# Moving two kinds of copies between ScalarE and VectorE, and replacing zero matmuls by wider ones, in an attention-then-MLP kernel

## The chip, the cores and the metric

The kernel runs on one core of one Trainium2 chip. The metric is device time in microseconds for one execution of the whole program; the time of a kernel is the median of several executions. Lower is better.

## The reference, cut to what matters

Eight batches, eight heads of 64, 512 tokens and 32 state rows. Two attentions without projections are computed for each head, one with the tokens as queries (`xread`) and one with the state rows as queries (`sread`), and all resulting rows go through one two-layer MLP with a SiLU.

```python
scores = scale * (x @ state.T)              # 512 x 32 for each batch and head
a = softmax(scores); xread = a @ state
a2 = softmax(scale * (state @ x.T)); sread = a2 @ x
rows = concat([xread, sread], axis=2) -> [4352, 512]
out = silu(rows @ w_in) @ w_out             # w_in 512x2048, w_out 2048x512
```

## The kernel before, in words

**The algebra.** Since `xread = a @ state`, the first MLP layer of a batch is `a @ (state @ w_in)`. So for each batch the kernel makes `W1 = state @ w_in` (`w1_m`, matmuls in line 282, copied out of PSUM by `w1_e`), the transposed softmax `aT`, then `g = silu(W1.T @ aT)` in 16 feature blocks (`g1`: matmuls in line 329, SiLU on ScalarE in line 338), and `out = g.T @ w_out` (`g2`, line 354; `G2` is one feature block for all four token tiles). The state reads of all batches are put through the MLP as a ninth batch (lines 341, 349).

**The softmax of a batch.** The tokens are cast to bf16 (`cast_x`), transposed on TensorE (`x_T`, line 144) and copied out (`x_Te`); `sc` (line 176) makes the scores, `ex` (line 187) the exponentials `en` on ScalarE, a VectorE reduction and a reciprocal give `rs`, and `norm_m`/`norm_g` (lines 202, 214) write the normalised `an`, part on VectorE and part on GpSimd (POOL). `a_T` (line 230) transposes `an` on TensorE into PSUM and copies it to `aT`. `sread_m` (line 246) makes the state reads.

**Order.** The whole schedule is written out by hand: each engine runs its instructions in the order of the Python calls, and a wait holds up all that stands behind it on that engine. `cp(eng, ...)` is the helper that puts a copy on VectorE (line 84), GpSimd (line 86) or ScalarE (line 88), so copies of many kinds share a line number. The eight PSUM banks have names (o0, o1, w0, w1, h0, h1, a0, a1), and a matmul into a bank waits for the copy that last reads it.

**The head (lines 386 to 506).** While the first tokens arrive by DMA, TensorE runs matmuls on a tile of zeros whose result nobody reads: `warm(n, bank, w)` issues n of them, each with its own weight load, w columns wide (128 if nothing is said).

```python
def warm(n, bk, w=128):
    for i in range(n):
        nc.tensor.matmul(bank[bk][:, 0:w], zeros[:, 0:128], zeros[:, 0:w], ...)
```

Then come batch 0's steps: `x_T(0, 0)` on the first two heads, `st_T` (line 124, the state's transpose, copied twice by VectorE into `sbd`), `st_f32` (an f32 copy `sbd_f`, one half on ScalarE), the other three `x_T`, `sc`, `ex`, and the reductions, with three more small `warm` calls between them. The first 512 columns of W1 are made in f32 straight from the loaded weights (`w1f_m`, line 295), in two halves around `a_T(0, ...)`.

**Batch 0 with batch 1 (lines 504 to 595).** `g1` and `G2` of batch 0 are interleaved with W1 pieces of both batches and with the softmax of batch 1. `load_wi(j)` and `load_wo(j)` bring 512-column pieces of the weights by DMAs that GpSimd issues. Near the end of this part ScalarE loads the table for the exponential, runs `ex(1, ...)` twice, loads the SiLU table back, and copies the last W1 piece of batch 0 (`w1_e(0, 3, HB, ...)`, from banks h0 and h1). `g1(0, 12)`, the next user of that piece, writes into bank h1. `a_T(1, ...)` stands behind it on TensorE.

**The rest (from line 598)** is a steady stream: batch k's `g2` matmuls with the next batch's work filled in between at fixed steps.

Of the kernel before, what the change touches and what calls it, by code (L numbers as in the profile page):

```python
# [19 lines left out]
def kernel(  # L20
# [58 lines left out]
    def bf(name):  # L79
        return bank[name][:].bitcast(BF16)  # L80

    def cp(eng, dst, src):
        if eng == "dve":
            nc.vector.tensor_copy(dst, src)  # L84
        elif eng == "pool":
            nc.gpsimd.tensor_copy(dst, src)  # L86
        else:
            nc.scalar.activation(dst, src, func=COPY, bias=0.0)  # L88
# [43 lines left out]
    def st_f32(bk, e0, e1):  # L132
        v = bf(bk)[:, 0:128]
        for half, e in ((0, e0), (1, e1)):
            cp(
                e,
                sbd_f[ds(64 * half, 64)],
                v[ds(64 * half, 64)].rearrange("p (ns kt) -> p kt ns", kt=KT),
            )

    def x_T(b, kt, bk):
        v = bf(bk).rearrange("p (k c t) -> p k c t", k=2, c=4)
        for c in range(4):
            nc.tensor.transpose(
                v[:, kt % 2, c, :], x_n[b % 2][:, kt, c, ds(2, 128)], ident[:]
            )
# [26 lines left out]
    def sc(b, kt, bk):  # L173
        v = bank[bk][:].rearrange("p (k h c s) -> p k h c s", k=2, h=2, c=4)
        for c in range(4):
            nc.tensor.matmul(  # L176
                v[:, kt % 2, :, c, :],
                xT[b % 2][:, kt, c, :],
                sbd[:, b, kt, :, :],
                start=True,  # L180
                stop=True,
                skip_group_check=True,
            )

    def ex(b, kt, n, bk):
        v = bank[bk][:].rearrange("p (k q s) -> p k q s", k=2, q=8)
        nc.scalar.activation(  # L187
            en[b % 2][:, :, :, ds(kt, n), :].rearrange("p h c k s -> p k (h c) s"),
            v[:, ds(kt % 2, n)],
            func=EXP,  # L190
            bias=0.0,
            scale=SCALE,
        )
# [6 lines left out]
    def norm_m(b, eng, kt=0, n=4, h0=0, hn=2):  # L200
        e = nc.vector if eng == "dve" else nc.gpsimd
        e.tensor_tensor(  # L202
            an[b % 2][:, ds(h0, hn), :, ds(kt, n), :].rearrange("p h c k s -> p (h c) k s"),
            en[b % 2][:, ds(h0, hn), :, ds(kt, n), :].rearrange("p h c k s -> p (h c) k s"),
            rs[b % 2][:, ds(h0, hn), :, ds(kt, n)]
            .rearrange("p h c k -> p (h c) k")
            .unsqueeze(3)
            .to_broadcast([128, 4 * hn, n, NS]),
            op=MULT,
        )  # L210

    def norm_g(b, eng, kt, n, q0, qn):
        e = nc.vector if eng == "dve" else nc.gpsimd
        e.tensor_tensor(
            an[b % 2][:].rearrange("p h c k s -> p (h c) k s")[:, ds(q0, qn), ds(kt, n), :],
            en[b % 2][:].rearrange("p h c k s -> p (h c) k s")[:, ds(q0, qn), ds(kt, n), :],
            rs[b % 2][:]
            .rearrange("p h c k -> p (h c) k")[:, ds(q0, qn), ds(kt, n)]
            .unsqueeze(3)
            .to_broadcast([128, qn, n, NS]),  # L220
            op=MULT,
        )

    def a_T(b, bks):
        n = 2 // len(bks)
        for i, (bk, e) in enumerate(bks):
            v = bf(bk).rearrange("p (h c t) -> p h c t", h=2, c=4)
            for half in range(n):
                for c in range(4):
                    nc.tensor.transpose(  # L230
                        v[:, half, c, :], an[b % 2][:, i * n + half, c, :, :], ident[:]
                    )
            cp(e, aT[b % 2][:, ds(i * n, n)], v[:, ds(0, n)])
# [22 lines left out]
    def sread_c(b, bk, o=0, eng="act"):  # L256
        cp(eng, s_f[b % 2][:], bank[bk][:, ds(o, 2 * D + 2)])
# [21 lines left out]
    def w1_m(b, j, bks, kts=range(KT)):  # L279
        for kt in kts:  # L280
            for half in range(2):
                nc.tensor.matmul(  # L282
                    bank[bks[half]][ds(32 * kt, 32), :],
                    sbd[ds(64 * half, 64), b, kt, half, :],
                    w_in_sb[ds(64 * half, 64), kt, ds(512 * j, 512)],
                    start=True,
                    stop=True,
                    skip_group_check=True,
                    tile_position=(64 * half, 32 * kt),
                )  # L290
# [14 lines left out]
    def w1_e(b, j, bks, engs, c0=0, n=512):  # L305
        for half in range(2):
            dst = W1[b % 2][:, half, ds(512 * j + c0, n)]
            src = bank[bks[half]][:, ds(c0, n)]
            if j > 0:
                dst = dst.rearrange("p (c q) -> p c q", c=4)  # L310
                src = src.rearrange("p (q c) -> p c q", c=4)
            cp(engs[half], dst, src)
# [38 lines left out]
    def g2(b, tt, ft, bk, cols=(0, 512)):  # L351
        src = g[b % 2] if b < B else g_s
        c0, c1 = cols
        nc.tensor.matmul(  # L354
            bank[bk][:, c0:c1],
            src[:, ft, ds(128 * tt, 128)],
            w_out_sb[:, ft, c0:c1],
            start=(ft == 0),
            stop=(ft == 15),
            skip_group_check=True,  # L360
        )
# [15 lines left out]
    def warm(n, bk, w=128):  # L377
        for i in range(n):
            nc.tensor.matmul(  # L379
                bank[bk][:, 0:w], zeros[:, 0:128], zeros[:, 0:w], start=True, stop=True,  # L380
                skip_group_check=True,
            )

    with tc.manual_schedule():
# [10 lines left out]
        for i in range(2):  # L395
            nc.vector.memset(x_n[i][:, :, :, 1:131:129], 1.0)
        nc.scalar.preload_act_table(EXP)
        warm(30, "o0")

        XB = ("o0", "o1", "o0", "w1")  # L400
        SB = ("h0", "h1", "a0", "a1")
# [1 line left out]
        HB = ("h0", "h1")  # L403
        OB = ("w0", "w1", "o0", "o1")
        DA = ("dve", "act")
        DD = ("dve", "dve")

        def G2(b, ft):
            for tt in range(4):
                g2(b, tt, ft, OB[tt])  # L410
# [37 lines left out]
        st_T(0, "w0", "dve", "dve")  # L448
        cast2(0, 2)
        st_f32("w0", "act", "dve")  # L450
        warm(3, "w1")
        x_T(0, 1, XB[1])
        x_Te(0, 1, 1, XB[1], "act")
        cast2(0, 3)
# [2 lines left out]
        load_wi(1)  # L457
        sc(0, 0, SB[0])
        ex(0, 0, 1, SB[0])
        warm(4, "w1")  # L460
        sc(0, 1, SB[1])
        ex(0, 1, 1, SB[1])
        x_T(0, 2, XB[2])
# [4 lines left out]
        x_Te(0, 3, 1, XB[3], "dve")  # L468
        rec(0)
        norm_m(0, "pool", 0, 2)  # L470
        warm(2, "o1")
        for kt in (2, 3):
            sc(0, kt, SB[kt])
            ex(0, kt, 1, SB[kt])
# [14 lines left out]
        warm(2, "o1", 512)  # L489
        nc.scalar.preload_act_table(SILU)  # L490
        w1_e(0, 0, ("w0", "w1"), ("act", "dve"), 0, 256)
        a_T(0, (("a0", "dve"), ("a1", "act")))
        sread_c(0, "o0", 0, "dve")
        cp("act", st_nat[:, 1, :], st_f[1][:])
        load_x(1, nc.gpsimd, 2, 2)
# [53 lines left out]
        norm_s(1, 0, 2)  # L549
        norm_m(1, "pool", 0, 2)  # L550
        nc.vector.tensor_reduce(rs[1][:, :, :, 2:4], en[1][:, :, :, 2:4, :], axis=AX, op=ADD)
        nc.vector.reciprocal(rs[1][:, :, :, 2:4], rs[1][:, :, :, 2:4])
        norm_g(1, "dve", 2, 2, 0, 5)
        norm_g(1, "pool", 2, 2, 5, 3)
        G2(0, 9)
        G2(0, 10)
        w1_m(0, 3, HB)
        w1_e(0, 3, HB, ("act", "act"))
        G2(0, 11)
        sread_m(1, "a0")  # L560
        g1(0, 12)
# [164 lines left out]
```

The softmax here doesn't subtract the row's maximum and nothing guards it: scores larger than these inputs give would overflow.

## Time and profile before

| | us |
|---|---|
| median of 5 executions | 215.96 (215.64 to 216.15) |
| the profiled execution | 215.37 |
| span in its trace | 213.6 |
| TensorE matmuls busy | 208.0 (97% of the span) |
| ScalarE busy | 135.6 (63%) |
| VectorE busy | 85.8 (40%) |
| GpSimd busy | 44.6 (21%) |

The span is the part of the profiled execution that the trace covers; 1.8 us lie around it. PE is TensorE's matmuls, PEld its weight loads, DVE is VectorE, ACT is ScalarE, POOL is GpSimd, SP issues most DMAs. In a timeline, each line gives the start and the duration in us, the engine, the source line, the operation, its output and input tiles, and how often it occurs; in brackets stands how long the engine had been idle and what released it. Matmuls overlap: the next one starts before the one before it has ended. In the chain of waits, the work that ended last is followed back from the end, each piece with its start and length. The granted TensorE clock is shown as full (9 in tenths) through the whole span.

### The profile page before, as it was taken

To read this page: it belongs to the slowest core of one execution; us is meant where nothing else is said; L and a number is where in the kernel's file an instruction comes from. 1 tells how busy PE (TensorE), PEld (TensorE's weight loads), DVE (VectorE), ACT (ScalarE), POOL (GpSimd) and SP (SyncE) were. 2 spreads that over 40 slices of the span, in tenths; PEclk is the share of its full clock that TensorE was granted. 3 is DMA by queue.
4 is the path that set the end of the run, shared out by engine and by line. 5 is a ranking of instruction groups with operands and counts; after the bars stand their busy time and mean duration, and the time that the engine had idled before them with its cause. 6 is when DMAs were issued, how large, how long until landed. Compare 5 with 4: busy or idle time off the path is not lost.

```text
span 213.6 us, 4128 instructions
## 1 busy us (share of the span) xinstructions
PE 208.0 (97%) x1666; PEld 104.6 (49%) x1666; DVE 85.8 (40%) x183; ACT 135.6 (63%) x227; POOL 44.6 (21%) x86
## 2 busy tenths in 40 slices
PE   7899999999999999999999999999999999999993
PEld 7544544444454454444444544444444444666553
DVE  4983758706801664076016741382027601111110
ACT  3856686789587668883886477846885476233211
POOL 3686249003400430052005200160001000000000
PEclk9999999999999999999999999999999999999999
DMA  6999997791780197119910891165014101111112
GB/s 200 324 253 271 235 287 76 183 292 68 166 275 9 45 197 248 49 49 155 290 49 0 205 248 48 49 166 129 3 49 112 55 34 49 52 49 49 49 52 98
DMA packets 36803, 27.86 MB, mean 130 GB/s; under 512 B 22064, under 2 KB 31152, under 8 KB 36784
## 3 DMA queue, kind: packets, MB, share of 16 engines
q1 hardware_dynamic: 31872, 21.63, 36.0%
q0 software_dynamic: 4208, 5.44, 12.2%
q10 hardware_dynamic: 704, 0.52, 0.7%
q8 instruction: 13, 0.21, 0.4%
q14 instruction: 6, 0.05, 0.1%
HBM read 17.30 MB, written 8.91 MB: 123 GB/s over the span
## 4 chain that ended last, share of the span: by engine, by line
PE 93%; ACT 3%; DVE 1%; issue 1%; ACTq 0%
PE ps_o L354 28%; PE ps_w L354 26%; PE ps_h L329 26%; PE ps_h L341 3%; PE ps_o L379 2%; PE ps_a L176 1%; ACT en L187 1%; PE ps_h L282 1%; PE ps_o L282 1%; PE ps_o L246 1%; ACT W L88 1%; PE ps_a L282 1%; PE ps_a L329 1%; ACT L548 1%; PE ps_w L282 1%
## 5 line engine op out<-in xcount | busy, mean ns | idle before, releaser
L338 ACT ACTIVATE g<-ps_h 128x512 bf16<-128x512 f32 x125 | 74.1, 597 | 32.5 <-PE ps_h L329 27.9
L354 PEld LDWEIGHTS <-g 128*128 128x128 bf16 x512 | 49.0, 98 | 55.3 <-issue 2.8
L329 PE MATMUL ps_h<-aT,W 128*128 128x512 bf16 x250 | 73.5, 379 | 0.3 <-ACT W L88 0.2
L354 PE MATMUL ps_w<-w_out_sb,g 128*128 128x512 bf16 x256 | 73.0, 379 | 0.1
L354 PE MATMUL ps_o<-w_out_sb,g 128*128 128x512 bf16 x256 | 66.7, 379 | 0.1
L329 PEld LDWEIGHTS <-W 128*128 128x128 bf16 x256 | 24.3, 98 | 27.6 <-issue 1.7
L202 POOL TENSOR_TENSOR an<-en,rs 128x512 bf16<-128x512 bf16 x8 | 8.4, 1053 | 107.9 <-ACT en L187 71.3
L84 DVE COPY o_sb<-ps_w 128x512 f32<-128x512 f32 (+1 forms) x13 | 8.5, 662 | 51.4 <-PE ps_w L354 51.4
L84 DVE COPY o_sb<-ps_o 128x512 f32<-128x512 f32 x14 | 9.5, 687 | 28.6 <-PE ps_o L354 28.5
L86 POOL CAST x_u<-x_f 128x256 bf16<-128x256 f32 x44 | 17.9, 451 | 0.0
L349 ACT ACTIVATE g_s<-ps_h 128x256 bf16<-128x256 f32 x16 | 6.1, 383 | 14.0 <-PE ps_h L341 14.0
L197 DVE TENSOR_REDUCE rs<-en 128x16 f32<-128x512 bf16 x13 | 8.6, 659 | 16.0 <-ACT en L187 15.9
L341 PE MATMUL ps_h<-xsT,w_in_sb 128*128 128x256 bf16 x64 | 9.6, 273 | 0.0
L88 ACT ACTIVATE W<-ps_h 128x512 bf16<-128x512 f32 x11 | 6.5, 598 | 3.7 <-PE ps_h L282 3.7
L341 PEld LDWEIGHTS <-w_in_sb 128*128 128x128 bf16 x64 | 6.9, 110 | 3.7
L88 ACT ACTIVATE o_sb<-ps_o 128x512 f32<-128x512 f32 (+1 forms) x4 | 2.2, 544 | 10.3 <-PE ps_o L354 7.9
L187 ACT ACTIVATE en<-ps_a 128x512 bf16<-128x512 f32 (+1 forms) x16 | 8.4, 568 | 0.5 <-PE ps_a L176 0.4
L176 PEld LDWEIGHTS <-xT 128*128 128x128 bf16 x128 | 5.9, 98 | 4.3 <-ACT xT L88 0.8
L640 ACT ACT_TABLE_LOAD x6 | 7.7, 1283 | 0.1
L187 ACT ACT_TABLE_LOAD x6 | 7.7, 1283 | 0.1
L84 DVE CAST W<-ps_h 128x512 bf16<-128x512 f32 x9 | 6.2, 683 | 4.0 <-PE ps_h L282 4.0
L88 ACT ACTIVATE o_sb<-ps_w 128x512 f32<-128x512 f32 (+1 forms) x5 | 2.7, 533 | 7.8 <-issue 6.2
(90 smaller groups left out, 173.8 us busy)
## 6 DMA issues: line engine op xcount, KB each, us to landing
out_dram<-o_sb SPq DMA_DIRECT2D x32, 256.0 KB, 2.6
x_f<-in_x_dram SPq DMA_DIRECT2D x8, 512.0 KB, 4.9
x_f<-in_x_dram SPq DMA_DIRECT2D x8, 256.0 KB, 4.5
w_in_sb<-in_moe_w_in_dram POOLq DMA_DIRECT2D x3, 512.0 KB, 9.4
w_out_sb<-in_moe_w_out_dram POOLq DMA_DIRECT2D x3, 512.0 KB, 9.5
w_f<-in_moe_w_in_dram SPq DMA_DIRECT2D x2, 512.0 KB, 5.8
wo_f<-in_moe_w_out_dram SPq DMA_DIRECT2D x4, 256.0 KB, 7.2
x_f<-in_x_dram POOLq DMA_DIRECT2D x2, 512.0 KB, 7.7
```

The lines of the kernel that those rows point to most:

```text
L84: nc.vector.tensor_copy(dst, src)
L86: nc.gpsimd.tensor_copy(dst, src)
L88: nc.scalar.activation(dst, src, func=COPY, bias=0.0)
L176: nc.tensor.matmul(v[:, kt % 2, :, c, :], xT[b % 2][:, kt, c, :], sbd[:, b, kt, :, :], start=True, stop=True, skip_group_check=True,)
L187: nc.scalar.activation(en[b % 2][:, :, :, ds(kt, n), :].rearrange("p h c k s -> p k (h c) s"), v[:, ds(kt % 2, n)], func=EXP, bias=0.0, sc ...
L197: nc.vector.tensor_reduce(v, en[b % 2][:, :, :, ds(kt, n), :], axis=AX, op=ADD)
L202: e.tensor_tensor(an[b % 2][:, ds(h0, hn), :, ds(kt, n), :].rearrange("p h c k s -> p (h c) k s"), en[b % 2][:, ds(h0, hn), :, ds(kt, n), ...
L282: nc.tensor.matmul(bank[bks[half]][ds(32 * kt, 32), :], sbd[ds(64 * half, 64), b, kt, half, :], w_in_sb[ds(64 * half, 64), kt, ds(512 * j, ...
L329: nc.tensor.matmul(bks[i][:], W1[b % 2][:, half, ds(128 * (f0 + i), 128)], aT[b % 2][:, half, :, :], start=(half == 0), stop=(half == 1), ...
L338: nc.scalar.activation(g[b % 2][:, f0 + i, :], bks[i][:], func=SILU, bias=0.0)
L341: nc.tensor.matmul(bk[:, 0:256], wi_cols(kt, ft), xsT[:, kt, :, :, :], start=(kt == 0), stop=(kt == KT - 1), skip_group_check=True,)
L354: nc.tensor.matmul(bank[bk][:, c0:c1], src[:, ft, ds(128 * tt, 128)], w_out_sb[:, ft, c0:c1], start=(ft == 0), stop=(ft == 15), skip_group ...
```

## The change

Three edits.

1. The zero matmuls: 30 of 128 columns become 8 of 512; 3 of 128 become 1 of 256; 4 of 128 become 1 of 512; 2 of 128 become 1 of 256. They are 39 before and 11 after, and their columns go from 4992 to 5120. The four other wide ones in the head are untouched.
2. In `a_T(0, ...)` the first half of the transposed softmax (bank a0) is copied by ScalarE and the second (bank a1) by VectorE; it was the other way round.
3. The last W1 piece of batch 0 is copied by VectorE (h0) and ScalarE (h1); both were on ScalarE. To do so the three lines that end batch 1's normalisation (one reciprocal on VectorE, `norm_g` on VectorE, `norm_g` on GpSimd) move behind the calls of `G2(0, 9)`, `G2(0, 10)`, `w1_m` and `w1_e`. On TensorE the order of instructions stays as it was but for the zero matmuls; on GpSimd and SP nothing changes place. On VectorE one copy of 128x512 is put in ahead of the reciprocal.

```diff
-        warm(30, "o0")
+        warm(8, "o0", 512)
...
-        warm(3, "w1")
+        warm(1, "w1", 256)
...
-        warm(4, "w1")
+        warm(1, "w1", 512)
...
-        warm(2, "o1")
+        warm(1, "o1", 256)
...
-        a_T(0, (("a0", "dve"), ("a1", "act")))
+        a_T(0, (("a0", "act"), ("a1", "dve")))
...
         nc.vector.tensor_reduce(rs[1][:, :, :, 2:4], en[1][:, :, :, 2:4, :], axis=AX, op=ADD)
+        G2(0, 9)
+        G2(0, 10)
+        w1_m(0, 3, HB)
+        w1_e(0, 3, HB, DA)
         nc.vector.reciprocal(rs[1][:, :, :, 2:4], rs[1][:, :, :, 2:4])
         norm_g(1, "dve", 2, 2, 0, 5)
         norm_g(1, "pool", 2, 2, 5, 3)
-        G2(0, 9)
-        G2(0, 10)
-        w1_m(0, 3, HB)
-        w1_e(0, 3, HB, ("act", "act"))
         G2(0, 11)
         sread_m(1, "a0")
         g1(0, 12)
         a_T(1, (("a1", "dve"),))
```

`DA` is ("dve", "act").

## The prediction

> **What bounds the kernel now.** I read the page's chain by engine first, then the chain in order of time for the first 32 us, then the timelines of the two places that the change touches, then the waits of TensorE.
>
> ```profile
> PE 93%; ACT 3%; DVE 1%; issue 1%; ACTq 0%
> ```
>
> TensorE carries nearly the whole span. After 12 us it hardly waits: in the stretch 36 to 100 us it is busy 63.81 of 64.00. So a delay or a gain that reaches TensorE at 12 us or at 31 us is carried to the end one for one, unless a wait in between takes it up. The head, in the chain of waits:
>
> ```profile
> 1.19 3.38 PE ps_o L379 x30
> 4.57 0.43 PE ps_o L144 x4
> 5.00 0.12 PE ps_w L124
> 5.12 0.02 issue
> 5.14 0.28 DVE sbd L84
> ```
>
> The 30 zero matmuls are themselves the first link. The first transpose starts at 4.36, right behind them, though its last input, the POOL cast (3.44 + 0.52), is ready at 3.96. From there the chain goes through the state's transpose, two VectorE copies, ScalarE's `sbd_f` and second `xT` copy, and by scores, exponentials and reductions to 9.08, where TensorE becomes dense. Two waits of TensorE matter, one from the list for matmuls and one from that for weight loads (us in total, times, longest):
>
> ```profile
> PE ps_h L329 <- ACT W L88: 0.2, 1, 0.2
> ```
>
> ```profile
> PEld L282 <- DMA w_in_sb<-in_moe_w_in_dram: 0.5, 1, 0.5
> ```
>
> The first is `g1(0, 12)` at 31.36, waiting for ScalarE's second W copy; edit 3 addresses it. The second is the W1 matmul at 21.25, the first to use weight piece 2.
>
> **Edit 1, the zero matmuls.** 30 of them take from 1.19 to the next start at 4.36: 3.17 us, 0.1057 each at 128 columns. Later the pace is twice as high: eight transposes at 25.00 take 0.45, 0.056 each. The change of pace falls near 6.2 us: the transposes at 4.36 last 0.31 each, one at 6.77 0.22. The granted clock reads 1.00 in both, so I go by pace. No row shows a 512-wide matmul at the slow pace. From above: four times the 128-wide row, 4 x 0.1057 = 0.423, and 8 x 0.423 = 3.38, that is 0.21 later than now. From below: the warm 512-wide row, 0.217 from start to start, 8 x 0.217 = 1.74; then the casts bound the transpose at 3.96 + 0.05, and VectorE's next cast (4.51 to 4.80), which stands ahead of the `sbd` copies, bounds those at 4.80 instead of 5.14: 0.34 earlier. I take +0.21, since its row is of the same matmuls in the same microseconds. Fewer instructions save nothing here: their weight loads lie under the matmuls already, and 8 x 512 = 4096 columns are more than 30 x 128 = 3840.
>
> [...]
>
> The three small ones: 3 x 128 to 256 columns frees TensorE 0.11 sooner for the second `x_T`, but ScalarE copies its result at 6.01 only after `sbd_f` (the chain), so nothing comes of it. 4 x 128 to 512 and 2 x 128 to 256 have the same columns, and behind each TensorE waits for ScalarE's `xT` (0.32 and 0.47 idle on the weight loads). These waits are the cover; without them the three would be worth -0.11 to 0.
>
> **What takes up the delay on the way.** The chain from 4.36 to 9.08 has no link that starts on a DMA, so +0.21 arrives at 12 us. At 21.25 the first W1 matmul starts 0.35 after the last `G2` matmul (20.90); the three others of its kind start 0.30 to 0.31 after theirs (15.85 to 16.15, 29.09 to 29.40, 33.32 to 33.62). So about 0.05 there is waiting for the weights. Their DMA was issued at 13.04 behind POOL casts that wait for DMAs, not for TensorE, so it lands when it did: -0.05. The same wait caps any gain in the head: what comes earlier to 21.25 waits there.
>
> **Edit 2, the swapped copies.** Now VectorE copies half 0 from 10.94 to 11.36 and ScalarE half 1 from 11.16 to 11.76. Swapped, with the same durations: ScalarE 10.94 + 0.60 = 11.54, VectorE 11.16 + 0.42 = 11.58. `g1(0, 0)` reads half 0 from 11.68, where TensorE comes from the `w1f_m` matmuls without a gap, and half 1 two matmuls later. The cover is those matmuls (11.08 to 11.68), with 0.14 less a hop of 0.05 to spare; if it were gone, half 0 would be 0.18 late. Next on VectorE stands `s_f` (11.50 instead of 11.28) and then the W copy at 11.86, which waits for TensorE anyway. I take 0; bounds 0 to +0.18 (nothing is late now, so there is nothing to gain).
>
> **Edit 3, the last W1 piece.** The timeline before:
>
> ```profile
> 29.35 0.63 DVE L551 TENSOR_REDUCE rs<-en 128x16 f32<-128x512 bf16 x1
> 29.58 1.05 POOL L202 TENSOR_TENSOR an<-en,rs 128x512 bf16<-128x512 bf16 x1 [5.00 <-DVE rs L198]
> ...
> 30.01 0.25 DVE L552 RECIPROCAL rs<-rs 128x16 f32<-128x16 f32 x1
> ...
> 30.22 1.08 ACT L88 ACTIVATE W<-ps_h 128x512 bf16<-128x512 f32 x2
> 30.30 0.69 DVE L214 TENSOR_TENSOR an<-en,rs 128x320 bf16<-128x320 bf16 x1
> 30.60 0.75 POOL L214 TENSOR_TENSOR an<-en,rs 128x192 bf16<-128x192 bf16 x1
> ...
> 31.36 0.59 PE L329 MATMUL ps_h<-aT,W 128*128 128x512 bf16 x2 [0.23 <-ACT W L88]
> ```
>
> ScalarE cannot start before 30.22 (table load). With one copy instead of two it is done at 30.82, and VectorE, starting at 30.01 with 0.69 for the same cast elsewhere, at 30.70. TensorE's weight load for `g1(0, 12)` already stood at 31.06, so that g1 moves from 31.36 to 31.06: -0.30. But behind it stands `a_T(1)`, at 31.79 now, and it reads what VectorE normalises. VectorE's next instruction starts 0.60 after such a cast (34.17, then 34.77), so reciprocal and `norm_g` come 0.60 later: `norm_g` ends at 30.90 + 0.69 = 31.59, and with a hop of 0.06 (copy end 26.18 to the weight load at 26.23) the transposes start at about 31.66. TensorE would be there at 31.06 + 2 x 0.217 = 31.49. So 0.17 of the 0.30 is given back to a **new wait**, on VectorE: -0.13 remains. POOL's part starts 0.15 after the reciprocal (29.43 to 29.58), at 31.01, and ends at 31.76; the sixth transpose, the first to read it, comes at 31.66 + 5 x 0.056 = 31.94, so it just hides. Behind POOL's `norm_g` are the state loads and the casts `x_u` of batch 2 (35.61 to 37.15), 0.41 later; VectorE's own half of these casts ends at 37.50, so the DMA transpose at 37.67 moves by 0.1 at most, and its result is not read before 44.16, over 2 us after a landing (4.4 typical). Bounds of edit 3: -0.30 with no new wait; +0.10 if the POOL part ends 0.3 later than worked out and holds the sixth transpose.
>
> **The sum.** 215.37 + 0.21 - 0.05 + 0 - 0.13 = 215.40 for the profiled execution. That one lies 0.59 below the median shown; the difference of +0.03 carries over, 215.96 + 0.03, about 216.0.
>
> **Rivals.** A measurement of this kernel can tell about 0.2% (0.43 us) from no change.
>
> *A later change of pace (slower).* If TensorE stays at the slow pace until about 9.6 us, the links of the chain between 6.2 and 9.6 pay: the third `x_T` 4 x 0.05 = 0.20, two score groups 0.09 each (0.31 against 0.22 for one matmul), the state read, 0.35 from its start to the next matmul, as much again: 0.73 in all, 216.7. [...] It decides if the pace changes later than about 8.5; a change at 7 costs under 0.2.
>
> *The gains alone (faster).* The head hides, because first data land later in timed executions than in the profiled one or because the pace is high sooner, and edit 3 gives its whole 0.30: -0.30, with an early head up to -0.64; middle 215.5. Against it: the wait for weight piece 2 caps the head's part at about 0, and the VectorE order makes the new wait almost certain.
>
> *A dearer new wait (no change).* Edit 3 at +0.10, the swap up to +0.18, head +0.16: 216.2 to 216.4, about where no change ends. The zero matmuls doing nothing but lengthen the head is in the forecast itself.
>
> **How the numbers follow.** Forecast 216.0: 0.53. Dearer wait: 0.12, of which all but 0.01 is no change. Later pace: 0.18 slower. Gains alone: 0.17, of which 0.16 over 0.2%. So faster 0.16, within 0.2% 0.65, slower 0.19. The range takes in the gains alone to 215.4 (edit 3 whole, half of the low end of the head) and the later pace with some noise of the median: 215.4 to 216.8; outside are the deepest early head and a pace later than 9.6.
>
> **What would show it.** In the changed trace: eight zero matmuls about 0.42 apart and the first transpose at about 4.57 to 4.60; `g1(0, 0)` about 0.21 later than 11.68 with no wait ahead; the W1 matmul after `G2(0, 5)` 0.30 behind its predecessor; no wait of `g1(0, 12)` on ScalarE, but one of the transposes in line 230 on VectorE's `an`, of 0.1 to 0.2. Wrong would be: the first transpose at 4.0, scores of the third group at the slow pace, or transposes of line 230 waiting on POOL.

## The result, and the profile after

| | before | after |
|---|---|---|
| median, us | 215.62 (88 runs) | 216.45 (48 runs) |
| ratio to before | | 1.0036, 95% interval 1.0025 to 1.0046 |
| profiled execution, us | 215.37 | 215.88 |
| span in its trace, us | 213.6 | 214.1 |

The change makes the kernel slower by 0.36%, more than the 0.2% that can be told from no change. The forecast was 216.0 and no change; the measured time lies inside the range, but on the slower side, which had been given a chance of 0.19. The profiled execution of the changed kernel is the fastest of its 48, so its trace shows less of the loss (0.5 us of span) than the medians (0.83).

The head came out nearly as worked out. In the chain of waits of the changed kernel (start, length, work):

```profile
1.20 3.59 PE ps_o L379 x8
4.79 0.43 PE ps_o L144 x4
5.22 0.12 PE ps_w L124
...
5.36 0.28 DVE sbd L84
```

The first transpose starts at 4.58 instead of 4.36, and `sbd` at 5.36 instead of 5.14: 0.22 late. `g1(0, 0)` follows at 11.86, 0.18 late, and the W1 matmul behind `G2(0, 5)` at 21.39, 0.14 late. Then the part that edit 3 changes, as a timeline (start, length, engine, line, operation):

```profile
30.03 0.67 DVE L84 CAST W<-ps_h 128x512 bf16<-128x512 f32 x1
30.36 0.60 ACT L88 ACTIVATE W<-ps_h 128x512 bf16<-128x512 f32 x1
...
30.62 0.24 DVE L556 RECIPROCAL rs<-rs 128x16 f32<-128x16 f32 x1
...
30.90 0.49 DVE L214 TENSOR_TENSOR an<-en,rs 128x320 bf16<-128x320 bf16 x1
...
31.21 0.61 PE L329 MATMUL ps_h<-aT,W 128*128 128x512 bf16 x2
...
31.65 0.22 PE L230 MATMUL ps_a<-ident,an 128*128 128x128 bf16 x1
```

`g1(0, 12)` no longer waits for ScalarE, and the transposes of line 230 start at 31.65 instead of 31.79. Seen from the W1 matmul at 21 us, which is 0.14 late, edit 3 gained 0.28. At 52 us the changed kernel is 0.14 **ahead**: the W1 matmuls of batch 2 start at 52.13 instead of 52.27. Everything that was argued about has happened by then, and the total is a gain. The loss comes after. The chain of waits there:

```profile
51.75 0.65 issue
52.40 0.74 POOL x_u L86
53.15 3.96 DMA aT<-an
...
57.15 0.60 PE ps_h L329 x2
```

The DMA transpose of batch 2's softmax, issued at 53.15, lands after 3.96 us. In the kernel before it is issued at 53.28 and lands after 3.1 (the list of what touches the tile `aT` from 52 to 58 us; the first line ends with the issue):

```profile
L236 SPq DMA_TRANSPOSE aT<-an x1: 1238/1238/1238, 53.3 to 53.3; - x1
...
DMA to landing us min/median/max: 3.1/3.1/3.1
```

The first `g1` of batch 2 waits for it and starts at 57.15 instead of 56.80. The chain by engine, which had no DMA in it before, now reads:

```profile
PE 92%; DMA 2%; DVE 2%; ACT 2%; issue 1%; POOL 0%; POOLq 0%; ACTq 0%
```

What the DMA engines moved from 50 to 60 us, in 40 slices of 0.25 us, first before, then after:

```profile
GB/s 0 0 369 434 246 0 0 0 0 66 0 0 0 0 0 0 0 13 201 220 207 207 275 393 385 197 0 0 182 217 209 207 215 220 214 217 186 206 114 135
```

```profile
GB/s 0 188 401 410 49 0 0 0 0 0 0 0 0 0 0 0 0 173 209 180 23 6 9 10 176 293 420 385 263 210 214 210 214 219 212 220 221 204 166 72
```

Before, the transpose's packets flow at about 200 GB/s from 54.5 without a break, and an output write follows. After, they begin at 54.25 and nearly stop from 55.0 to 56.0 (23, 6, 9, 10). Ahead of the stall one thing lies elsewhere, the lone 66 at 52.25 in the first row: a single packet of 16 KB on the queue marked "instruction". In the changed kernel it comes in the slice from 54.25 to 54.5 (packets, MB, and the time that they took as a share of 16 engines' time):

```profile
q1 hardware_dynamic: 105, 0.03, 51.0%
q8 instruction: 1, 0.02, 25.4%
```

From that line the packet's own length can be worked out: 25.4% of 16 engines' 0.25 us is 1.0 us, about as long as the transpose's packets stall.

That queue has 13 packets and 0.21 MB in the whole span, 16 KB each. The profile of the kernel before counts 1666 matmuls and 1666 weight loads on TensorE, 3332 instructions; that of the changed one 1638 of each, 56 fewer. (Of the zero matmuls it lists 42 before and 14 after, so the untouched wide ones are three, not four.) From the first packet to the last (13.05 to 205.16 before, 13.99 to 210.23 after) TensorE runs 2919 instructions in the kernel before and 3003 in the changed one, for 12 packets each: one for 243 and one for 250 on average, at uneven distances. No row names the engine that the packets are for; that they are loads of TensorE's code is the author's reading, and the experiments below, where their places change with TensorE's instruction count (52.3 to 53.9 in e8, which has 30 fewer and nothing else changed), are what speaks for it. With 56 instructions fewer, from the head, the packets behind it fall at other places in the schedule: the fourth at 54.3 instead of 52.3, the fifth at 77.7 instead of 71.2. (The 3286, 3278 and 3246 instructions of the expectations below stand in no view; their differences, 8 and 40, are those of the profiles.)

### The profile page after: what moved, and what is told of

Read it like the earlier page. It is cut to its first block, busy times and chain, and to the rows that moved or that the text cites. A ratio compares the mean times of both kernels' runs of the same rounds, so it can differ in the third digit from the quotient of the medians.

```text
span 214.1 us, 4083 instructions
## 1 busy us (share of the span) xinstructions
PE 208.0 (97%) x1638; PEld 101.7 (47%) x1638; DVE 85.4 (40%) x184; ACT 135.2 (63%) x226; POOL 44.7 (21%) x86
## 4 chain that ended last, share of the span: by engine, by line
PE 92%; DMA 2%; DVE 2%; ACT 2%; issue 1%; POOL 0%; POOLq 0%; ACTq 0%
PE ps_o L354 27%; PE ps_h L329 26%; PE ps_w L354 25%; PE ps_h L341 3%; PE ps_o L379 2%; DMA aT<-an 2%; PE ps_a L176 2%; PE ps_h L282 1%; PE ps_o L282 1%; PE ps_o L246 1%; PE ps_a L282 1%; ACT en L187 1%; PE ps_a L329 1%; ACT L187 1%; PE ps_w L282 1%
## 5 line engine op out<-in xcount | busy, mean ns | idle before, releaser
L84 DVE CAST W<-ps_h 128x512 bf16<-128x512 f32 x10 | 6.8, 682 | 3.9 <-PE ps_h L282 3.9
L88 ACT ACTIVATE W<-ps_h 128x512 bf16<-128x512 f32 x10 | 6.0, 598 | 3.6 <-PE ps_h L282 3.6
```

## The experiments

In what follows a code load is such a packet, and landing is the time from a transfer's issue to its arrival.

**Theory (code):** the change's 56 fewer TensorE instructions move one code load to where it disturbs batch 2's DMA transpose. **Rivals:** the copies moved by edits 2 and 3 do it, by changing when the transpose is issued (order); or the wide zero matmuls cost more than their 0.2 us in the head (width, columns).

**e1_copies_only**: edits 2 and 3 with the old zero matmuls.

```diff
-        warm(8, "o0", 512)
+        warm(30, "o0")
```

and likewise for the three small ones. 

> Edits 2 and 3 alone; the zero matmuls are those of before, so TensorE has its 3286 instructions again. Code theory (the fewer TensorE instructions move one 16 KB load of TensorE's code from 52.3 us, ahead of batch 2's DMA transpose of aT, to 54.3 us, into it, and that transpose lands 0.9 later): the load is back near 52.3, aT lands in 3.1 us, no wait of line 329 on it, and the time is before less the gain at 31 us: -0.25 to -0.35, about 215.3. Order theory (the late transpose comes from the copies being moved, which make its issue 0.14 earlier): aT still lands in 4.0 and the time is above before by 0.3 to 0.4. Width theory (the loss lies in the wide zero matmuls in the head): -0.3 too, but with nothing to see at 54 us.

Measured 216.16 against 215.76, ratio 1.001 (0.9986 to 1.0034): the time alone decides nothing. The trace does: load at 52.5, transpose landed in 3.1, no wait on it. The gain of edit 3 did not show in this execution, since a `G2` matmul waited for `w_out` until 26.8, which ate it.

**e2_zeros_only**: edit 1 alone (all four lines of zero matmuls), the copies as before. 

> Edit 1 alone, copies as before. Code theory: 56 instructions fewer, so the load falls near 54.5, aT of batch 2 lands in about 4 us; +0.19 from the head, less 0.05 at the weights, +0.6 from the transpose: +0.7 to +0.8, slower than the full change by the 0.28 that edit 3 brings. Order theory: aT lands in 3.1, +0.14. Width theory: above before by more than 0.3, all of it ahead of 12 us.

Measured 216.62 against 215.76, ratio 1.0040 (1.0016 to 1.0064). Load at 54.5, the transpose landed in 4.1 us and was waited for. Order falls: no copy was moved here, and the transpose is late. Width falls too: the W1 matmuls of batch 2 start at 52.21, 0.06 ahead of the kernel before, so nothing of the loss lies in the head.

**e3_32x128**: the full change, its first zero matmuls cut finer.

```diff
-        warm(8, "o0", 512)
+        warm(32, "o0")
```

> The full change with its first zero matmuls cut as 32 of 128 instead of 8 of 512: the same 4096 columns and the same time in the head, but 3278 TensorE instructions, 8 fewer than before instead of 56. Code theory: load near 52.5, no stall, before -0.14, about 215.5, that is 0.6 to 0.9 faster than the full change. Order theory and a pure column count: as the full change, 216.4.

Measured 215.76 against 215.76, ratio 0.9999 (0.9975 to 1.0024). The same columns at the same place, and the loss of the full change is gone. The load came at 54.0, later than expected, 0.6 ahead of the transpose's first packets (54.6); the packets slowed for only 0.5 us and landed in 3.3, and nobody waited. In the traced execution the head was late for another reason: the matmuls of line 295 stood 0.7 us. The profile names ScalarE's `st_nat`, but they read the second half of `w_f`, which landed at about 11.4 (issued at 4.2, 7.2 to landing), and started at 11.55. So the transpose was issued at 53.4, 0.3 later than in the full change, and one trace can't tell how often the load leaves it in peace; the time is that of 12 executions.

**e4_16x256**: the same with 16 of 256. 

> The full change with 16 zero matmuls of 256: the same 4096 columns, 3246 instructions, 40 fewer than before. Code theory: the load falls between 52.5 and 54.3; a stall of 0.6 if it still meets the transpose (packets from about 54.25 on), none (before -0.14) if it is over by then; either way the wait of line 329 goes with the position of the load. Order theory and a pure column count: as the full change, 216.4.

Measured 216.72 against 215.76, ratio 1.0036 (1.0012 to 1.0061). Load at 54.9, in the midst of the packets; the transpose landed in 4.3.

**e8_before_15x256**: the kernel before with nothing changed but this:

```diff
-        warm(30, "o0")
+        warm(15, "o0", 256)
```

> The kernel before with one line changed: its 30 zero matmuls of 128 columns are 15 of 256, the same 3840 columns, 30 TensorE instructions fewer; no copy is moved. Code theory: the load that stands at 52.3 in the kernel before moves to 54 or later, batch 2's DMA transpose lands in about 4 us, and the time is 0.4 to 0.9 above before, about 216.2 to 216.5, with no difference at 50 us. Column theory (only more columns in the head cost): no change.

Measured 216.32 against 215.80, ratio 1.0038 (1.0015 to 1.0062). This is the cleanest one: the same columns, every copy where it was, 30 instructions fewer, and a loss of the same size. At 52 us its trace is 0.18 ahead of the kernel before. Load at 53.9; the waits of TensorE's matmuls (us in total, times, longest) have the new one beside the old:

```profile
PE ps_h L329 <- DMA aT<-an: 0.5, 1, 0.5
...
PE ps_h L329 <- ACT W L88: 0.2, 1, 0.2
```

and in its chain of waits the transpose is 4.09 long:

```profile
53.10 4.09 DMA aT<-an
...
57.24 0.60 PE ps_h L329 x2
```

The same trace has a second meeting. Batch 3's transpose is issued at 74.3 in e8 and in the full change alike. In e8 the next code load comes at 76.4, amid its packets; in the full change at 77.7, after it has landed. First e8, then the full change:

```profile
L236 SPq DMA_TRANSPOSE aT<-an x1: 1240/1240/1240, 74.3 to 74.3; - x1
...
DMA to landing us min/median/max: 4.7/4.7/4.7
```

```profile
L236 SPq DMA_TRANSPOSE aT<-an x1: 1239/1239/1239, 74.3 to 74.3; - x1
...
DMA to landing us min/median/max: 3.1/3.1/3.1
```

It costs e8 another 0.17 us: its matmuls are 0.45 behind the kernel before at 75 us and 0.62 at 90.

**e5_g1_later**: the full change with batch 2's `g1` started later, so that nothing waits for the late transpose.

```diff
-        2: (None, None, 70, (4,), 5, 111, 110, 1.2),
+        2: (None, None, 70, (4,), 5, 111, 114, 1.0),
```

> The full change, with batch 2's g1 started three steps later in the plan and set one step apart (start 111 to 114, spacing 1.2 to 1.0), so that the late transpose is no longer waited for. If the loss is that wait alone, the load still meets the transpose, which still lands late, but TensorE does not wait for it: 0.4 to 0.7 below the full change, 215.7 to 216.0; 0.1 to 0.3 of it may be lost again to ScalarE, which then has its SiLUs closer together. If the late transpose is only a sign of something that slows the whole kernel, as the full change: 216.4.

(In the plan's line for batch 2, the last two numbers are the start of `g1` and its spacing. The start moves by four steps, 110 to 114; the text on record says three.) Measured 217.18 against 215.80, ratio 1.0068 (1.0046 to 1.0089): a miss. The transpose was late as ever (4.4) and nothing waited for it, but the later SiLUs got behind batch 3's exponentials and both table loads on ScalarE, and a `g2` matmul waited 1.6 us for one. In the chain of waits:

```profile
70.98 1.28 ACT L640
...
72.28 0.61 ACT g L338
...
72.93 0.39 PE ps_w L354
```

So this run can't say whether the wait alone is the loss; it shows that the start of batch 2's `g1` has no room on the late side.

**e7_w1_only** and **e6_w1_swapped**: edit 3 alone, and edit 3 alone with its two engines changed over.

```diff
-        w1_e(0, 3, HB, DA)
+        w1_e(0, 3, HB, ("act", "dve"))
```

They are about a second, smaller loss that the traces of the full change, e1, e3 and e4 share: from batch 2's first `g1` to the state reads at 75 us (line 246) they take 18.27 or 18.28 us, the kernel before, e2 and e8 18.14 or 18.15. 

> Edit 3 alone. 0.28 gained at 31 us as in the trace of the full change, then about 0.13 lost from 58 to 68 us, where ScalarE's SiLUs of batch 2 each have one more semaphore instruction (28 on line 338 before, 40 in the full change): before -0.15. If the semaphore instructions cost nothing: -0.28. No meeting of load and transpose in either, since TensorE's instructions are those of before.

> Edit 3 alone with its two engines changed over: ScalarE copies h0 and VectorE h1. The program then has no second wait on the SiLUs of batch 2 (28 or 29 semaphore instructions on line 338). If those cost the 0.13: 57 to 75 us passes as fast as in the kernel before, and the time is before -0.28, that is 0.13 below edit 3 alone. If not: as edit 3 alone.

Measured: e7 215.69 against 215.80, ratio 1.0007 (0.9987 to 1.0026); e6 215.52, ratio 0.9994 (0.9972 to 1.0015). The times can't be told apart, from each other or from before. The traces can: e7 passes that stretch in 18.27, e6 in 18.14. The semaphore instructions on line 338 (count, then shortest, median and longest in ns), before, in the full change and in e6:

```profile
L338 ACTq EVENT_SEMAPHORE  x28: 17/17/567, 12.8 to 165.8; - x28
```

```profile
L338 ACTq EVENT_SEMAPHORE  x40: 17/17/3572, 13.6 to 166.3; - x40
```

```profile
L338 ACTq EVENT_SEMAPHORE  x29: 17/17/567, 13.1 to 166.0; - x29
```

The 12 more are all in batch 2 (16 there instead of 4). With VectorE on h0 its SiLUs wait on two semaphores each, TensorE's and ScalarE's own, and take an instruction more for it. In that stretch the SiLUs come back to back (0.60 us each, one every 0.64 to 0.70 from 57.4 to 60.1 in the kernel before), and four of the `g1` pairs of e1 are 0.47 long in the chain instead of 0.43, against one in the kernel before. (e7's profiled execution took 217.61, with matmuls waiting 1.2 us for `w_f` in the head; only the stretch is read from it.)

**All traces together**, by how far the code load lies ahead of the first packets of batch 2's transpose (both read in steps of 0.1 us; the whole trace of e7 is 2.1 late):

| kernel | TensorE instructions against before | load, us | first packets, us | landing, us |
|---|---|---|---|---|
| e7 | 0 | 54.3 | 56.5 | 3.1 |
| before | 0 | 52.3 | 54.4 | 3.1 |
| e6 | 0 | 52.5 | 54.6 | 3.1 |
| e1 | 0 | 52.5 | 54.5 | 3.1 |
| e3 | -8 | 54.0 | 54.6 | 3.3 |
| e8 | -30 | 53.9 | 54.2 | 4.1 |
| after | -56 | 54.3 | 54.3 | 4.0 |
| e5 | -56 | 54.3 | 54.2 | 4.4 |
| e2 | -56 | 54.5 | 54.3 | 4.1 |
| e4 | -40 | 54.9 | 54.2 | 4.3 |

2 us ahead, nothing happens; 0.3 ahead or later, 0.9 to 1.3 us are lost. The four kernels whose `g1` waited for it (after, e2, e4, e8) have a ratio of 1.0036 to 1.0040; those without a late transpose (e1, e3, e6, e7) 0.9994 to 1.0010.

The table leaves a rival: the five late transposes were also issued earliest, at 53.1 to 53.2 against 53.3 and later, so the moment of issue could be the cause. Batch 3 answers it: issued at 74.3 in both traces, with a load amid its packets 4.7, without one 3.1. That the load causes the stall rests on this pair, on e8, which changes one line and no column, and on the stall itself, which begins 0.5 to 1.0 us after the load's packet does in all five traces. How it does so inside the DMA engines no run shows, nor why the load's place does not move evenly with the count (it is later with 40 fewer than with 56 fewer). That the wait is the whole of the 0.83 between the medians is not shown: the trace of the full change accounts for 0.5 in one execution, and the waits seen (0.49 in the full change, 0.60 to 0.85 in e2, e4 and e8, against the kernel's own course up to there) make the rest likely.

## Why the prediction was right in its range and wrong in its mechanism

That 216.45 lies between 215.4 and 216.8 is luck. The upper part of the range was there for a later change of pace, and that is not what cost the time; the forecast itself, +0.03, was of no change.

- **Edit 1, execution in the head: right in the profiled execution.** Forecast +0.21, measured +0.22 at the first transpose and +0.18 at `g1(0, 0)`. In e2 and e4 the pace changed before the zero matmuls were through, the first transposes started at 4.33 and 4.27, and the casts bound what followed; `g1(0, 0)` came 0.02 earlier than before in e2 and 0.13 later in e4. "The chain from 4.36 to 9.08 has no link that starts on a DMA" is true of the one trace it was read from; e2's chain has the tokens' load in it, e4's the load of `w_f`.
- **Edit 1, when the pace changes:** in e4 the last two zero matmuls already start at 4.05 and after at the high pace, 2.9 us after the first one; the change of pace lies between 4.0 (e4) and 6.2 (before). No run shows what sets that moment, nor a slow pace until 9.6, the term of the slower rival.
- **"Fewer instructions save nothing here" is the step that failed.** It priced the 28 matmuls by their run time and weight loads, and not by their 56 places in TensorE's code. The missing term is +0.49 at 57 us in the trace. The profile before showed the queue ("instruction", 13 packets); the prediction gave these packets no place in time.
- **The weights at 21 us: right.** 0.05 forecast; 0.18 late at 11.86 became 0.14 late at 21.39.
- **Edit 2: right.** No wait around it in the full change.
- **Edit 3: right in kind, too small in gain.** Forecast -0.13, measured -0.28 in the full change. In all seven traces with edit 3 the matmuls gain 0.27 to 0.29 there, from 30.2 to 31.8 us, each against the same one before; in e1 and e7 a wait for `w_out` just ahead had cost more than that. The new wait of the transposes on VectorE, 0.17 by the forecast, did not come. The mis-sized term is VectorE's `norm_g`: it was given the 0.69 of the old trace, where it started beside POOL's `norm_m`, and takes 0.49 at its new place, so it ends at 31.39, and the transposes start at 31.65 right behind `g1(0, 12)`. Why it takes less there no run shows. Batch 0's row for six such groups, 0.56 for 384 elements, would have given 0.47 for these 320.
- **Edit 3, what was not thought of:** the order of two copies changed the waits that the program puts on later SiLUs, 12 semaphore instructions more, and +0.13 between 57 and 75 us.
- **"Carried to the end one for one, unless a wait in between takes it up"** looked only for waits that shorten a delay. Two new ones made it longer.
- **The rivals:** a later change of pace, the one on the slower side, had nothing to do with it. The right side had a chance of 0.19, for the wrong reason. Of the gains alone, the half on edit 3 came true (0.28 of its 0.30).

The sum of the trace: +0.19 head, -0.05 weights, -0.28 edit 3, +0.49 transpose, +0.14 SiLUs = +0.49; the span grew by 0.5.

## What to carry to other kernels

Here 30 to 56 instructions fewer on TensorE moved the code load at 52.3 us by 1.6 to 2.6 us and the next one from 71.2 to 76.4 (e8) and 77.7 (the full change). Before calling an edit of TensorE's instruction count free, find the packets of the instruction queue in the trace, ask which transfers with little slack lie near, and price what a late landing would hold up. If a kernel gets slower for no reason in the edited part, compare the two traces from the end of that part on, and undo the instruction count alone (same work, cut finer) as the first experiment. A head read from one trace has the bounds of one execution.

## What the runs showed of the hardware that was not expected

- One 16 KB code load, 0.3 us ahead of a DMA transpose's packets or amid them, makes the transpose land 0.9 to 1.3 us later (five traces), in e8's batch 3 1.6 later. 2 us ahead it does nothing (four traces), and neither does one at the very end: in the kernel before, batch 5's transpose, issued at 116.3, has a load at 118.7, 0.7 us ahead of its end, and lands after 3.1.
- TensorE's high pace (eight transposes in 0.45 us, 0.056 each, against 0.1057 for a zero matmul of 128 columns in the head) began from 2.9 (e4) to 5.0 us (before) after its first matmul, in different executions of almost the same head, while the mean granted clock read 0.999 or 1.000 over each span.
- Where SiLUs come back to back, a second semaphore on each, 17 ns by its own row, went with three more `g1` pairs of 0.47 instead of 0.43 us, and 0.13 us over batch 2.
